# Eight row places for the projection of token blocks 2 and 3, and attention dealt out anew

## The chip, the cores and the metric

The kernel runs on one core of a Trainium2 chip. A time is device microseconds (us) of one execution. The engines are called as in the profile: PE (TensorE, matrix products), DVE (VectorE), ACT (ScalarE), POOL (GpSimd) and SP (SyncE, which here only issues DMAs). PE, DVE, ACT, POOL and SP each work off their own queue of instructions in the order in which the program puts them there. Before the change three timed runs took 1111.26, 1112.67 and 1114.58 us; their median, 1112.67 us, is the time before. The forecast is for the same median of the changed kernel.

## What is computed

A parallel transformer block on 2048 tokens of width 576. The input is normalized; sliding dilated attention (32 heads of width 18, 8 keys at distances 0, 2, ... 14) and a feed-forward network with squared ReLU (width 4608) both work on it, and both results are added to the input.

```python
def _A_ref(x, wqkv, wo):
    qkv = (x @ wqkv).reshape(B, S, 3, H, Dh)          # H = 32, Dh = 18
    ...
    idx = pos[:, None] - off[None, :]                 # off = 0, 2, ..., 14
    logits = jnp.einsum("bhsd,bhswd->bhsw", q, kg) * scale
    attn = _softmax(jnp.where(mask, logits, -1e9), axis=-1)
    o = jnp.einsum("bhsw,bhswd->bhsd", attn, vg)
    return o.reshape(B, S, D) @ wo

def _B_ref(x, w1, b1, w2, b2):
    h = jnp.einsum("bsd,df->bsf", x, w1) + b1
    r = jnp.where(h > 0, h, 0)
    return jnp.einsum("bsf,fd->bsd", r * r, w2) + b2

xn = _layernorm(x)
return x + _A_ref(xn, A_wqkv, A_wo) + _B_ref(xn, B_w1, B_b1, B_w2, B_b2)
```

## The kernel before

**Tiling.** The tokens lie in four blocks of 512 (0 to 3), the heads in four groups of 8 (0 to 3). Products in fp32 are made of high and low parts, so each operand is split by ACT (a rounded copy) and DVE (the rest). Several products are made for two blocks at once with fewer, combined products (the names `T1`, `B11`, `T2`, `T3`, `B21`, `B22`, `T4`).

**Stages.** First Q, K, V of blocks 0 and 1 (`q0`). Then `phase_a(0)`: 18 pairs of FFN tiles (`ffn_pair`, p = 0 to 17) for blocks 0 and 1, with the second FFN product and the output of block 0 between them. Then `phase_b0`: the second FFN product of block 1 (36 tiles), then Q, K, V of blocks 2 and 3, which `quad_step` makes in four halves: `(k, half)` = (0, 0), (0, 1), (1, 0), (1, 1), where k = 0 is for groups 0 and 1 and k = 1 for groups 2 and 3. Each half has 14 steps `(s, i)`, in the order of the list `steps` (L1246). The last two steps of the fourth half stand in the first FFN pair of `phase_a(1)`, as does the output of block 1 (`filler`: the functions `o_hi`, `o_lo` turn and split what attention left, `chunks` makes the products). Then `phase_a(1)` does the same as `phase_a(0)` for blocks 2 and 3, and `phase_b1` the rest of block 3.

**Rows.** A step with s = 4, 5, 6 or 7 ends with a *row*: 128 tokens of K, V and Q of one group. `row` (L1103) has ACT copy it from a PSUM bank to a place in SBUF, has DVE add a second bank where there is one (s = 4 and 6), and sends it to the DRAM tensor `kvq` of its group. There are eight rows in a half, 32 in all. The place comes from `stage`: one tile `st` with four places (`open_stage`), so that row n and row n + 4 share a place; for rows 24 to 27 a second tile, in a buffer of the name `w1r`, is added in the fourth half. A row without a second bank is sent by ACT's queue, the others by SP's, and by POOL's from row 24 on.

**Attention** of a block and group is a generator (`attention`, L403) with some 18 pieces of DVE work between its `yield`s: for four token places a product of the query with eight keys and a sum over the head's width; the softmax, whose exponential is ACT's; then for four places a product with the values and three adds. `side(k)` (L449) runs k pieces where it stands in the program. `PIECES` says how many each FFN pair of `phase_a(0)` gets after its first products; `2 + p % 2` does so in `phase_a(1)`; a tuple in `quads` (L1251) says after which steps of a half one piece stands; `complete(b)` (L470) runs pieces until block b is done.

**Slots of keys and values.** K (with 14 tokens ahead) and V of a block and group each need a buffer named `kv`, of which there are three. `offer` puts a block and group in the list, `fetch` issues the loads on POOL's queue while a slot is free, `release` gives a slot back (after the last product with K, and after the last add with V). With `kept_back` at 1 one free slot is kept: it is for `regroup(1)` (L893), which loads what attention left of block 1, regrouped by head, for the output of block 1.

**Order.** Nothing is moved by a scheduler: each engine's order is the order in which the program writes its instructions.

Of the kernel before, what the change touches and what calls it, by code (L numbers as in the profile page):

```python
# [8 lines left out]
F32 = mybir.dt.float32  # L9
# [7 lines left out]
P = 128  # L17
# [25 lines left out]
NS = 7  # L43
PLAIN = 3
ROWS = {(4 * b - 1 + k // 3, k % 3): (b, h) for b in (2, 3) for k, h in ((0, 0), (2, 2), (3, 1), (5, 2), (6, 2))}
PIECES = (0, 1, 2, 2, 2, 2, 1, 3, 2, 2, 1, 1, 1, 2, 1, 2, 3, 3)
STACK = {T1: 0, B11: 1, B22: 2, B21: 3, T3: 4, T2: 5, T4: 6}


# [1 line left out]
def block_kernel(ctx: ExitStack, tc: tile.TileContext, x, xt, wqkv, wo, w1, b1, w2, b2, w1l, out):  # L51
# [13 lines left out]
    def kv_tile(n):  # L65
        return sb.tile([P, n], F32, name="kv", bufs=3)
# [286 lines left out]
    def open_stage():  # L353
        stage[0] = sb.tile([P, 2 * NS * P], F32, name="st")[:, :NJ * QW].rearrange("p (j c) -> p j c", c=QW)
# [35 lines left out]
    def release():  # L390
        free[0] += 1
        fetch()
# [76 lines left out]

    def complete(b):  # L470
        while due(b):
            left = side(1)
            assert not left or current[0] is None

    def run(gens, k):

# [172 lines left out]
    def ffn_pair(s, p, work, first=False):  # L649
# [96 lines left out]
            w1_again(n + 1, 0) if s else combine_w1(n + 1)  # L746
        part(0)
        if not first:
            side(2 + p % 2 if s else PIECES[p], False)
        work(0)  # L750
        product(bb, T2, ss(2))
        own_w2 = first and s == 1
# [77 lines left out]
    def phase_a(s, filler):  # L830
        b = 2 * s
        ffn_pair(s, 0, filler, first=True)
        open_y(b)
        for p in range(1, NP):
            h, ops = hs.pop(s * NP + p - 1), []

            def work(i):
                if i in (0, 2):
                    ops.extend(tile_products(b, 2 * p - 2 + i // 2, h))
                add(b, ops[7 * i:7 * i + 7])  # L840

            if p == NP - 1:
                complete(b)
                regroup(b, 0)
                regroup(b, 1)
                if s == 0:
                    residual(b)
                    load_xt(2)
            ffn_pair(s, p, work)
        if s:  # L850
            residual(b)
        else:
            release()
# [12 lines left out]
        open_left(b)  # L866
        o_hi(b, 3)
        o_lo(b, 2), o_lo(b, 3)
        add(b, tile_products(b, NF - 1, h))
        w2_hi()  # L870
        w2_lo()
        o_hi(b, 4)
        o_lo(b, 4)
        side(1)
        load_h(s, 1)
        load_left(b)
        for c in range(NC):
# [207 lines left out]
    def quad_step(k, s, j, i):  # L1085
# [15 lines left out]
                nc.tensor.matmul(to, v[:, js], ws[LEFT, f][:, n], start=False, stop=n == 1, skip_group_check=True)  # L1101

        def row(n, f, x, y=None):  # L1103
            places = stage[(rows_out[0] // NJ + 1) % len(stage)]
            st = places[:, rows_out[0] % NJ]
            rows_out[0] += 1
            nc.scalar.activation(st, x, AF.Copy)
# [3 lines left out]
            (nc.scalar if y is None else nc.sync if len(stage) < 2 else nc.gpsimd).dma_start(to, st.rearrange("p (i c) -> p i c", c=CG))  # L1111

        ss = lambda n: lambda h, q: SS[n][:, h, q]
        if s == 1:
# [26 lines left out]
    def phase_b0():  # L1141
# [35 lines left out]
                nc.sync.dma_start(yscr[:, c - 1:c + 1], xr[b][0][:, c - 1:c + 1])  # L1177
        nc.sync.dma_start(yleft, kept(b, NC - 1))
        open_stage()

        def fourth_slot(k):
            split_slot(T4, raw[k, 0][:, 0])

        def hook(k, half, s, i):
# [9 lines left out]
            if half and not k:  # L1194
# [32 lines left out]
                if (s, i) == (6, 1):  # L1227
                    split_side(1, 1)
                    split_slot(B22, b22)
                    kept_back[0] = 1  # L1230
                    for g in (0, 1):
                        offer(2, g)
            if half and k:
                if (s, i) == (3, 0):
                    stage[1] = sb.tile([P, NJ, QW], F32, name="w1r", bufs=2)
                if (s, i) == (2, 1):
                    w1_again(NP, 0, nc.sync)
                if (s, i) == (5, 1):
                    complete(1)
                if (s, i) == (4, 1):  # L1240
                    w1_again(NP, 1, nc.sync)
            if kept_back[0] and not due(1):
                regroup(b, 0)
                fetch()

        steps = [(1, 0), (1, 1), (2, 0), (2, 1), (3, 0), (3, 1), (5, 0), (4, 0), (5, 1), (4, 1), (7, 0), (6, 0), (7, 1), (6, 1)]  # L1246
        def quads(k, half, some):
            for n in some:
                s, i = steps[n]
                quad_step(k, s, 2 * half + i, i)  # L1250
                if n in ((2, 3, 4, 6, 8, 10, 12), (3, 6, 8, 10, 12, 13), range(1, 14), (3, 6, 8, 10))[2 * k + half]:  # L1251
                    side(1)
                hook(k, half, s, i)

# [430 lines left out]
```

## Time and profile before

| | |
|---|---|
| timed runs | 1111.26, 1112.67, 1114.58 us |
| profiled execution, its own time | 1109.8 us |
| its span, first to last instruction | 1108.0 us |
| PE busy | 1094.3 us, 99% of the span |
| DVE busy | 879.2 us, 79% |
| ACT busy | 562.8 us, 51% |
| POOL busy | 150.0 us, 14% |
| moved by DMA | 298.97 MB, mean 270 GB/s |

The profiled execution is 1.8 us longer than its span, and lies 2.9 us below the median of the timed runs. In rows of the profile `st<-p` means that `st` is written from `p`; `p` are the PSUM banks, `pr`, `lg`, `mx`, `sm`, `q` the tiles of attention, `kvq` the DRAM tensors of K, V and Q, `o` those of attention's results. A number in brackets is the time for which the engine was idle ahead of the row, with the work that ended it. Times in rows are counted from the span's start. L118 is the helper `tt`, DVE's work on two tensors. PEld is PE's loading of weights, SPq, ACTq the DMA-issuing side of a queue.

### The profile page before, as it was taken

Reading aid. Unit: us, or ns where it says so; the run is one execution under the profiler, and the core shown is the slowest. Engines: PE = TensorE matmul, PEld = TensorE weight load, DVE = VectorE, ACT = ScalarE, POOL = GpSimd, SP = SyncE. Lnnn points to the kernel's source line nnn. Section 1 sums busy time; section 2 is a strip of 40 time slices with the busy share of each in tenths; the row PEclk is TensorE's granted clock in tenths of the full one; section 3 lists DMA queues with packets and bytes.
Section 4 is the critical chain, followed back from the end, with each engine's and each line's share of the span. In section 5 each row is a group of like instructions: output and inputs, shape, how many; then the busy total and the mean of one; then the engine's idle time right before and its main releaser. Section 6 shows DMA issues by size and latency. Waiting matters only on the chain.

```text
span 1108.0 us, 13955 instructions
## 1 busy us (share of the span) xinstructions
PE 1094.3 (99%) x4936; PEld 923.6 (83%) x4936; DVE 879.2 (79%) x1183; ACT 562.8 (51%) x794; POOL 150.0 (14%) x267
## 2 busy tenths in 40 slices
PE   9999999999999999999997999999999999999998
PEld 7998888888888888888896988888888888888887
DVE  7687988898898978999877486675767676889955
ACT  5435665656656564555343355454555545533442
POOL 4000401031130201002010300210101010101010
PEclk9999999999999999999998999999999999999999
DMA  8966998889988998876753888869586868685572
GB/s 284 334 218 220 341 404 301 321 288 261 393 278 300 341 351 284 292 252 239 268 143 120 289 322 309 296 211 332 197 316 213 289 231 309 207 289 197 186 282 88
DMA packets 109558, 298.97 MB, mean 270 GB/s; under 512 B 12648, under 2 KB 42736, under 8 KB 98608
## 3 DMA queue, kind: packets, MB, share of 16 engines
q1 hardware_dynamic: 69984, 192.84, 48.7%
q0 software_dynamic: 13200, 62.52, 16.8%
q10 hardware_dynamic: 26304, 42.71, 11.7%
q8 instruction: 39, 0.64, 0.2%
q14 instruction: 31, 0.25, 0.1%
HBM read 213.53 MB, written 84.50 MB: 269 GB/s over the span
## 4 chain that ended last, share of the span: by engine, by line
PE 88%; DVE 5%; DMA 4%; ACT 1%; issue 1%; ACTq 0%; POOL 0%; DVEq 0%; POOLq 0%
PE p L568 44%; PE p L672 34%; PE p L1097 4%; DMA kvq<-st 3%; PE p L365 2%; PE p L1101 1%; PE p L678 1%; DVE w1r L118 1%; DVE w1s L118 1%; DVE pr L118 1%; PE p L1460 1%; DVE r L118 1%; DVE lg L414 0%; DMA w2r<-in_w 0%; ACT st L357 0%
## 5 line engine op out<-in xcount | busy, mean ns | idle before, releaser
L568 PE MATMUL p<-h,w2s 128*128 128x512 f32 x2066 | 491.7, 389 | 0.3 <-ACT h L718 0.2
L568 PEld LDWEIGHTS p<-h,w2s 128*128 128x128 f32 x2066 | 387.4, 188 | 82.1 <-ACT h L718 0.6
L672 PE MATMUL p<-X,w1s 128*128 128x512 f32 x864 | 219.5, 389 | 0.2 <-DVE w1s L118 0.2
L672 PEld LDWEIGHTS p<-X,w1s 128*128 128x128 f32 x864 | 162.1, 188 | 34.0 <-DVE w1s L118 0.6
L118 DVE TENSOR_TENSOR w2s<-w2r,w2s 128x576 fp32r<-128x576 f32 x164 | 123.5, 754 | 79.5 <-ACT w2s L541 79.2
L541 ACT ACTIVATE w2s<-w2r 128x640 fp32r<-128x640 f32 x164 | 120.2, 735 | 125.9 <-PE p L568 97.9
L672 PE MATMUL p<-S,w1s 128*128 128x512 f32 x648 | 164.5, 389 | 0.0
L672 PEld LDWEIGHTS p<-S,w1s 128*128 128x128 f32 x648 | 121.6, 188 | 25.1
L443 POOL DMA_DIRECT2D o<-q x128 | 69.5, 608 | 402.8 <-DVE q L118 401.2
L714 ACT ACTIVATE r<-r,b1t 128x512 f32<-128x512 f32 x72 | 52.1, 724 | 115.4 <-DVE r L118 112.3
L118 DVE TENSOR_TENSOR pr<-q,kv 128x1152 f32<-128x1152 f32 x64 | 86.7, 1354 | 1.0 <-DVE q L118 0.2
L414 DVE TENSOR_REDUCE lg<-pr 128x64 f32<-128x1152 f32 x64 | 86.4, 1351 | 1.0
L118 DVE TENSOR_TENSOR pr<-lg,kv 128x1152 f32<-128x1152 f32 x64 | 86.6, 1353 | 0.8
L118 DVE TENSOR_TENSOR pr<-pr 128x576 f32<-128x576 f32 (+1 forms) x128 | 77.6, 607 | 3.6
L722 ACT ACTIVATE r<-r 128x1024 f32<-128x1024 f32 x72 | 76.1, 1057 | 1.2
L118 DVE TENSOR_TENSOR r<-p,r 128x512 f32<-128x512 f32 (+1 forms) x77 | 53.1, 689 | 28.5 <-ACT r L780 14.7
L118 DVE TENSOR_TENSOR h<-r,h 128x1024 fp32r<-128x1024 f32 (+3 forms) x46 | 51.8, 1136 | 18.6 <-ACT r L722 9.7
L756 ACT ACTIVATE r<-p 128x512 f32<-128x512 f32 x36 | 21.5, 598 | 80.9 <-PE p L672 80.9
L118 DVE TENSOR_TENSOR w1s<-w1r,w1s 128x1024 fp32r<-128x1024 f32 (+2 forms) x42 | 46.2, 1103 | 10.4 <-ACT w1s L510 10.0
L714 ACT ACTIVATE r<-p,b1t 128x512 f32<-128x512 f32 x72 | 48.2, 671 | 1.5 <-DMA out<-r 1.5
L118 DVE TENSOR_TENSOR h<-h 128x1024 fp32r<-128x1024 f32 x36 | 43.9, 1220 | 2.1 <-ACT h L994 2.0
L118 DVE TENSOR_TENSOR w1r<-w1r 128x256 f32<-128x256 f32 (+5 forms) x69 | 40.8, 591 | 5.4 <-ACT w1r L585 3.9
(204 smaller groups left out, 1173.8 us busy)
## 6 DMA issues: line engine op xcount, KB each, us to landing
w2r<-in_w SPq DMA_DIRECT2D x144, 320.0 KB, 4.2
kv<-kvq POOLq DMA_DIRECT2D x30, 1296.0 KB, 8.5
w<-w1s SPq DMA_DIRECT2D x21, 1024.0 KB, 8.8
w1s<-w ACTq DMA_DIRECT2D x19, 1024.0 KB, 7.5
h<-r SPq DMA_DIRECT2D x36, 512.0 KB, 7.0
h<-h SPq DMA_DIRECT2D x36, 512.0 KB, 4.1
w<-w1s SPq DMA_DIRECT2D x15, 768.0 KB, 12.1
w1s<-w ACTq DMA_DIRECT2D x15, 768.0 KB, 5.0
```

The source lines that it names most:

```text
L118: return nc.vector.tensor_tensor(out=out, in0=a, in1=b, op=op)
L365: nc.tensor.matmul(p[:, :QW], l, r, start=k == 0, stop=k == len(mm) - 1)
L414: nc.vector.tensor_reduce(out=lg[:, j * HG:(j + 1) * HG].rearrange("p a w -> p w a"), in_=pr.rearrange("p w (a d) -> p w a d", d=DH), axis ...
L443: nc.gpsimd.dma_start(rows[:, i], q[i * L:(i + 1) * L, :, a:z])
L541: nc.scalar.activation(w2s[stream[i]][:, :DE], raw2[i], AF.Copy)
L568: nc.tensor.matmul(yp[b][c], v, a, start=c not in yb[b], stop=c in last and c not in [o[0] for o in ops[i + 1:]], skip_group_check=True)
L672: nc.tensor.matmul(to, l, r, start=start and i == 0, stop=i == len(mm) - 1, skip_group_check=True)
L678: nc.tensor.matmul(to, weight(LEFT, k, f), v, start=False, stop=k == 1, skip_group_check=True)
L714: nc.scalar.activation(to, a, AF.Relu, bias=b1t[:, f:f + 1])
L722: nc.scalar.activation(r, r, AF.Square)
L756: nc.scalar.activation(u[:, 0], bb, AF.Copy)
L1097: nc.tensor.matmul(to, l[:, js], r, start=start and n == 0, stop=n == len(mm) - 1, skip_group_check=True)
```

## The change

1. **Places.** After the second FFN product of block 1, `phase_b0` takes one of the three `kv` slots as second tile of `stage`, for rows 0 to 3, 8 to 11 and 16 to 19; `st` holds rows 4 to 7, 12 to 15, 20 to 23, and 28 to 31 as before; rows 24 to 27 go to the `w1r` buffer as before. Row n and row n + 8 share a place. The queues that send the rows are as before.
2. **Slots.** One slot is kept back from the end of `phase_a(0)` to the start of the projection, so that it is there; during the projection attention has two slots, up to step (3, 0) of the fourth half, where the third is given back and `kept_back` goes to 1.
3. **Pieces.** In the third half the piece after step 2 is left out; in the fourth half the four pieces are left out, and `complete(1)` is called at step (3, 0) in place of (5, 1) alone. FFN pair 13 of `phase_a(0)` gets 0 pieces in place of 2, pair 14 gets 2 in place of 1. In `phase_a(1)` a pair gets `2 + (p > 2)` in place of `2 + p % 2`: pair 1 one less, the even pairs from 4 on one more.
4. `complete` ends with the last piece of a block; before, `side(1)` in it went on to the first piece of the next.

```diff
-PIECES = (0, 1, 2, 2, 2, 2, 1, 3, 2, 2, 1, 1, 1, 2, 1, 2, 3, 3)
+PIECES = (0, 1, 2, 2, 2, 2, 1, 3, 2, 2, 1, 1, 1, 0, 2, 2, 3, 3)
...
     def complete(b):
         while due(b):
-            left = side(1)
-            assert not left or current[0] is None
+            if current[0] is None:
+                assert not side(1)
+            else:
+                current[1] = next(current[0], "end")
+                if current[1] == "end":
+                    current[0] = None
...
-            side(2 + p % 2 if s else PIECES[p], False)
+            side(2 + (p > 2) if s else PIECES[p], False)
...
         else:
+            kept_back[0] = 1
             release()
...
-            places = stage[(rows_out[0] // NJ + 1) % len(stage)]
+            places = stage[(rows_out[0] // NJ + 1) % 2]
...
-            (nc.scalar if y is None else nc.sync if len(stage) < 2 else nc.gpsimd).dma_start(...)
+            (nc.scalar if y is None else nc.gpsimd if "last" in stage else nc.sync).dma_start(...)
...
         open_stage()
+        assert free[0]
+        free[0] -= 1
+        kept_back[0] = 0
+        stage[1] = kv_tile(NJ * QW).rearrange("p (j c) -> p j c", c=QW)
...
                     split_slot(B22, b22)
-                    kept_back[0] = 1
                     for g in (0, 1):
                         offer(2, g)
             if half and k:
                 if (s, i) == (3, 0):
-                    stage[1] = sb.tile([P, NJ, QW], F32, name="w1r", bufs=2)
+                    stage[1] = stage["last"] = sb.tile([P, NJ, QW], F32, name="w1r", bufs=2)
+                    kept_back[0] = 1
+                    free[0] += 1
+                    complete(1)
...
-            if kept_back[0] and not due(1):
+            if kept_back[0] and "last" in stage and not due(1):
                 regroup(b, 0)
                 fetch()
...
-                if n in ((2, 3, 4, 6, 8, 10, 12), (3, 6, 8, 10, 12, 13), range(1, 14), (3, 6, 8, 10))[2 * k + half]:
+                if n in ((2, 3, 4, 6, 8, 10, 12), (3, 6, 8, 10, 12, 13), (1, *range(3, 14)), ())[2 * k + half]:
                     side(1)
```

PE's order is the same in both programs, row for row. The line numbers of the changed program are up to 11 higher (L1107 is L1112 there, L1111 is L1116).

ACT, at the end of the second half and in the third: the row copies `st<-p` (L1107), the exponential `lg<-lg` (L423) of the attention of block 1, group 0, and the copies between banks (L1116, L1121). Before:

```order
L1107 ACTIVATE st<-p_4850 128x432
L122 ACTIVATE r_5172<-mb 128x432
L122 ACTIVATE h<-w1r 128x2x432
L1116 ACTIVATE p_4838<-p_4837 128x432
L1116 ACTIVATE p_4849<-p_4848 128x432
L1121 ACTIVATE p_4840<-p_4838 128x432
L423 ACTIVATE lg<-lg 128x256
L1121 ACTIVATE p_4851<-p_4849 128x432
L1107 ACTIVATE st<-p_4837 128x432
L1111 DMA kvq_98<-st 128x3x144
L1107 ACTIVATE st<-p_4838 128x432
```

The changed program there:

```order
L1112 ACTIVATE st<-p_4849 128x432
L122 ACTIVATE r_5173<-mb 128x432
L122 ACTIVATE h<-w1r 128x2x432
L1121 ACTIVATE p_4837<-p_4836 128x432
L1121 ACTIVATE p_4848<-p_4847 128x432
L1126 ACTIVATE p_4839<-p_4837 128x432
L1126 ACTIVATE p_4850<-p_4848 128x432
L423 ACTIVATE lg<-lg 128x256
L1112 ACTIVATE kv<-p_4836 128x432
L1116 DMA kvq_98<-kv 128x3x144
L1112 ACTIVATE kv<-p_4837 128x432
```

The exponential stands one copy later, straight ahead of the third half's first row copies, and those go to the `kv` tile.

DVE, in the third half: the end of the softmax, and the first of the row adds (from the bank of step (4, 0)) among the products with the values. Before:

```order
L425 TENSOR_REDUCE sm<-lg 128x32
L426 RECIPROCAL sm<-sm 128x32
L118 TENSOR_TENSOR lg<-lg,sm 128x256
L118 TENSOR_TENSOR pr<-lg,kv 128x1152
L118 TENSOR_TENSOR st<-p_4839,st 128x432
```

The changed program there:

```order
L425 TENSOR_REDUCE sm<-lg 128x32
L426 RECIPROCAL sm<-sm 128x32
L118 TENSOR_TENSOR lg<-lg,sm 128x256
L118 TENSOR_TENSOR kv<-p_4838,kv 128x432
L118 TENSOR_TENSOR pr<-lg,kv 128x1152
```

The row add has moved ahead of the product with the values, and so have the three that follow it.

POOL, from the end of `phase_a(0)` to the fourth half, tiles with their numbers: Q, K and V loads of group 1 and group 0 (`kvq1`, `kvq0`), the stores of attention's results of block 1 (`o10`, `o11`). The tiles `q_3841`, `kv_3840`, `kv_4712` are Q, K, V of block 1, group 0 before; `q_5195`, `kv_5194` are Q and K of block 2, group 0. Before:

```order
L387 DMA kv_3731<-kvq1_97 128x2592
L443 DMA o10_102<-q_3062 128x1x96 x4
L443 DMA o11_103<-q_3062 128x1x48 x4
L385 DMA q_3841<-kvq0_96 128x576
L387 DMA kv_3840<-kvq0_96 128x2592
L607 DMA stk1_152<-st_4232 32x4x128 x14
L387 DMA kv_4712<-kvq0_96 128x2592
L443 DMA o10_102<-q_3494 128x1x96 x4
L443 DMA o11_103<-q_3494 128x1x48 x4
L385 DMA q_5195<-kvq0_96 128x576
L387 DMA kv_5194<-kvq0_96 128x2592
```

The changed program there:

```order
L443 DMA o10_102<-q_3140 128x1x96 x4
L443 DMA o11_103<-q_3140 128x1x48 x4
L387 DMA kv_3838<-kvq1_97 128x2592
L611 DMA stk1_152<-st_4228 32x4x128 x14
L385 DMA q_4709<-kvq0_96 128x576
L387 DMA kv_4708<-kvq0_96 128x2592
L443 DMA o10_102<-q_3570 128x1x96 x4
L443 DMA o11_103<-q_3570 128x1x48 x4
L387 DMA kv_4998<-kvq0_96 128x2592
L385 DMA q_5196<-kvq0_96 128x576
L387 DMA kv_5195<-kvq0_96 128x2592
```

Each load stands later: V of block 1, group 0 (`kv_4712` before, `kv_4998` now) is behind the stores of group 1's results, and K of block 2 (`kv_5195`) waits there for the slot of K of block 1, group 0.

More of the change, by code (lines that the diff above doesn't have):

```diff
@@ L1110, in row @@
             to = kvq[gs[f]][:, PAD + n * TB:PAD + (n + 1) * TB].rearrange("i (p j) c -> p j i c", j=NJ)[:, j]
-            (nc.scalar if y is None else nc.sync if len(stage) < 2 else nc.gpsimd).dma_start(to, st.rearrange("p (i c) -> p i c", c=CG))
+            (nc.scalar if y is None else nc.gpsimd if "last" in stage else nc.sync).dma_start(to, st.rearrange("p (i c) -> p i c", c=CG))
         ss = lambda n: lambda h, q: SS[n][:, h, q]
```

## The prediction

> **What bounds the kernel now.** I read first the page's busy times, then who PE waited for, then PE's busy time over the halves of the projection, then the chain of waits at the one place where it falls. Page, and the list of PE's waits (us in total, times, longest us):
>
> ```profile
> span 1108.0 us, 13955 instructions
> PE 1094.3 (99%) x4936; PEld 923.6 (83%) x4936; DVE 879.2 (79%) x1183; ACT 562.8 (51%) x794; POOL 150.0 (14%) x267
> ...
> PE p L1097 <- ACT st L1107: 7.2, 1, 7.2
> PE p L1377 <- DVE lg L1370: 2.1, 1, 2.1
> PE p L568 <- ACT h L718: 0.2, 1, 0.2
> PE p L672 <- DVE w1s L118: 0.2, 1, 0.2
> ```
>
> PE is the bound, and 13.7 us of the span are all that it isn't busy. Of these 2.1 lie at the start, and 7.2 in one wait for a row copy of the projection. PE's order isn't changed, so the change can gain or lose only by PE's waits. The halves of the projection, from the first matmul of one to that of the next (PE busy in the second column, then PEld, DVE, ACT, POOL, the granted clock, DMA share, GB/s):
>
> ```profile
> 542.70:562.28 19.58, 19.58 (x101) 18.82 (x100) 15.40 (x23) 7.32 (x13) 0.00 (x0) 1.00 0.76 244
> 562.28:581.86 19.58, 19.58 (x101) 18.82 (x100) 16.32 (x19) 10.40 (x18) 5.45 (x10) 1.00 0.42 113
> 581.86:610.41 28.55, 21.30 (x102) 20.02 (x101) 21.05 (x30) 8.61 (x17) 0.00 (x0) 0.88 0.36 114
> ```
>
> Three halves with the same matmuls: two take 19.58 us, the third 28.55. The excess, 28.55 - 19.58 = 8.97 us, is more than the wait of 7.2: the clock granted in the third is 0.88, and PE is busy 21.30 us for work of 19.58. A stall of 7.25 us and 1.72 us at a lower clock after it make the 8.97. Where it comes from, by the chain of waits (start, length, what) and the timeline there:
>
> ```profile
> 579.12 0.60 DVE st L118
> ...
> 579.74 12.37 DMA kvq<-st
> ...
> 592.21 0.54 ACT st L1107
> ...
> 578.44 0.57 POOL L385 DMA_DIRECT2D q<-kvq  x1 [9.68 <-DMA kvq<-st]
> 579.00 0.56 POOL L387 DMA_DIRECT2D kv<-kvq  x1
> 581.47 0.93 ACT L122 ACTIVATE h<-w1r 128x864 fp32r<-128x864 f32 x1 [0.44 <-ACT st L1107]
> 582.30 0.55 ACT L122 ACTIVATE r<-mb 128x432 fp32r<-128x432 f32 x1
> 585.58 0.60 DVE L118 TENSOR_TENSOR r<-mb,r 128x432 fp32r<-128x432 f32 x1
> 592.78 0.61 DVE L118 TENSOR_TENSOR st<-p,st 128x432 f32<-128x432 f32 x1 [6.60 <-ACT st L1107]
> 592.80 5.24 PE L1097 MATMUL p<-w1s,S 128*128 128x432 f32 x18 [7.25 <-ACT st L1107]
> ```
>
> Row 11 is finished by DVE at 579.72 and sent at 579.74, behind the loads of Q and K that POOL issued at 578.44 and 579.00; it lands 12.37 us later. Row 15 uses the same place of `st`, so its copy, which ACT comes to at 582.85 behind two splits, starts at 592.21; it is the copy that empties the bank which PE's next product overwrites. DVE, too, stands idle for 6.60 us.
>
> **Part 1, the places: -8.97 us.** With a reuse distance of eight, row 15 waits for row 7. That was finished here:
>
> ```profile
> 563.90 0.60 DVE L118 TENSOR_TENSOR st<-p,st 128x432 f32<-128x432 f32 x1
> ```
>
> Sent at 564.5, it would have to take over 18 us to hold a copy at 582.85; the slow one took 12.37. Row 23 follows row 15 by one half, 19.58 us: the same margin. So the wait goes, and with it the low clock. Taken away whole: 8.97 us.
>
> The Trainium skill (TensorE: Matmul & The Clock Gate, Part 1: The HAM clock gate) says that an idle window of about 3.4 us halves the clock, and about 3.4 us of busy time restore it; by that rule the ramp costs 1.7 us, as the rows have it, and waits under some 3 us left by the change would cost no ramp.
>
> **Part 2, DVE and ACT in the third half: 0 to +0.3 us.** PE comes 8.97 us earlier, DVE only the 6.60 that it stood idle: the add of row 15 follows the row of 585.58 at once. So against PE, DVE is 2.4 us later in the third half than before. Who waits for it:
>
> ```profile
> 599.75 0.42 ACT L423 ACTIVATE lg<-lg 128x256 f32<-128x256 f32 x1 [2.34 <-DVE lg L118]
> 600.52 0.51 ACT L1107 ACTIVATE st<-p 128x432 f32<-128x432 f32 x1
> 601.53 0.53 ACT L1107 ACTIVATE st<-p 128x432 f32<-128x432 f32 x1 [0.50 <-PE p L1097]
> 604.14 1.33 PE L1097 MATMUL p<-h,X 128*128 128x432 f32 x6
> 614.80 0.31 DVE L118 TENSOR_TENSOR q<-pr 128x144 f32<-128x144 f32 x1
> ```
>
> The exponential waits for DVE, and two row copies are queued behind it on ACT; the second empties the bank of the product at 604.14 (step (7, 0)). Now: exponential at 599.75 - 6.60 = 593.15, ending at 593.57; the copy between banks that followed it is done earlier, so the first row copy starts then, the second 1.01 after it, as here (594.58), and ends at 595.11. PE comes to (7, 0) at 604.14 - 8.97 = 595.17. That holds by 0.06 us; I charge 0 to 0.3 and take 0.1. The row adds stand ahead of the products with the values now, so the later steps have more room than this one.
>
> **Part 3, what attention left of block 1 comes later: 0 to +4 us.** The attention of block 1, group 0 ends at 615.11 before; now at 615.11 - 6.60 and 0.2 more (the moved add, due at 594.9, waits for the copy that ends at 595.11), so 608.7. PE's shift would have put it at 606.1: it is 2.6 us late. Behind it stand the results' stores, the load of V, the regrouping load, the turning, and chunk 0 of block 1's output on PE. Timeline, and the landing times of the regrouping loads:
>
> ```profile
> 622.29 0.54 POOL L901 DMA_DIRECT2D kv<-o  x1 [0.57 <-DMA o<-q]
> ...
> DMA to landing us min/median/max: 12.0/13.8/15.5
> ...
> 637.85 1.30 DVE L925 STREAM_TRANSPOSE r<-kv 128x512 f32<-128x512 f32 x2 [0.64 <-DMA kv<-o]
> 639.31 1.14 ACT L926 ACTIVATE h<-r 128x512 fp32r<-128x512 f32 x2
> 641.58 12.86 PE L568 MATMUL p<-h,w2s 128*128 128x512 f32 x56
> ...
> 620.00:640.00 20.00, 20.00 (x97) 17.86 (x96) 6.99 (x10) 7.40 (x14) 5.24 (x8) 1.00 1.03 354
> ```
>
> The first load is issued 7.18 us after attention's end and takes 15.5 us, with all DMA engines full (share 1.03). Now: issued at 615.9; at the same 15.5 it lands at 631.4, and one turn (0.65) and one split (0.57) later, at 632.6, PE has what it needs. PE comes there at 641.58 - 8.97 = 632.61. Lower bound: the load finds fewer transfers ahead of it, since those that PE triggers moved by 8.97, and lands up to 2.6 us earlier: no wait. Upper bound: the longest landing of a row's store, 19.6 us (quoted below), so a wait of 4.1. I take 0.2, nearest to this load's own 15.5.
>
> The skill (DMA: Bandwidth & Descriptors, Queues, rings and completion order) says that each DMA engine takes its queues in turn, packet by packet. By it POOL's queue keeps its share however late the load is issued, and lands in the same 15.5 us; the sum stays.
>
> **Part 4, loads with two slots: 0.** V of group 0 can only be loaded once V of group 1 is done with:
>
> ```profile
> 567.70 1.07 POOL L443 DMA_DIRECT2D o<-q  x2 [0.15 <-issue]
> 621.16 0.56 POOL L387 DMA_DIRECT2D kv<-kvq  x1 [1.41 <-DMA o<-q]
> ...
> 601.50 1.36 DVE L118 TENSOR_TENSOR pr<-lg,kv 128x1152 f32<-128x1152 f32 x1
> ...
> DMA to landing us min/median/max: 5.6/8.8/17.6
> ...
> DMA to landing us min/median/max: 2.1/4.0/19.6
> ```
>
> The stores end at 568.77; the load follows by 570.2 (POOL's wait of 1.41 at the same place of the next attention, 621.16), and by the landing times of all such loads (first of the two rows; the second is the rows' stores) it lands between 575.8 and 587.8. DVE needs it at 601.50 - 6.60 and, behind the moved add (0.2 and 0.6), so at 595.7: 7.9 us of room at the worst. Row stores that it now runs beside are waited for by nobody for eight rows. K of block 2 waits for the slot of K of block 1, and is first read in the next FFN pair, behind the turned results of 632. V of group 1 and K of group 0 are loaded during block 1's second FFN product, long before use.
>
> **Part 5, the other pieces: 0.** Pieces in FFN pairs 13 and 14 move by two at most, 2.7 us at 1.36; PE waits on DVE in no pair there (0.2 us in all, above). In `phase_a(1)` seven even pairs get a piece more. Four pairs of 17.4 us, DVE's busy time alone:
>
> ```profile
> 700.00:717.45 17.45, 11.42 (x12) 1.00 0.88 311
> 717.45:734.90 17.45, 12.18 (x17) 1.00 0.75 271
> 734.90:752.40 17.50, 12.24 (x15) 1.00 0.63 210
> 752.40:769.80 17.40, 11.42 (x12) 1.00 0.91 322
> ```
>
> Over 5 us of each are free, so a piece of 1.36 fits, and odd pairs have three already. Without that cover it would be 7 x 1.36 = 9.5 us.
>
> **Sum.** -8.97 + 0.1 + 0.2 = -8.67 us. The profiled execution took 1109.8, so 1101.1; the median of the runs is 2.9 above that, and I put the gain on the median: 1112.67 - 8.67 = 1104.0.
>
> **The rivals.**
>
> *A, given back at chunk 0.* The regrouping load lands late, by part 3's upper bound: PE idles 4.1 us there and, if the ramp is paid again, 1.7 more. Net gain 8.67 + 0.2 - 5.8 = 3.1, so 1109.6; half of it, 1106.9, is the middle. For: two steps without slack, and DMA full. Against: the transfers it competes with start 8.97 us earlier. Chance 0.16, of it 0.03 below the 0.3% mark.
>
> *B, slower: DVE stuck for V of group 0.* Every row add and the exponential are queued behind that product on DVE. From 595.7 on, after some 0.8 us of slack (taken small), each us that V lands later is a us of PE. To be past the old time by 0.3% (3.3 us) it must cost 12.0, so land after 608.5, 38 us after its issue; the longest such landing is 17.6. For: it runs beside eight row stores, and one store took 12.37 beside such a load. Time 1116 or more. Chance 0.05.
>
> *C, DVE becomes the bound in `phase_a(1)`.* 9.5 us back: 1113.5, no difference. For: three pieces ahead of the first products. Against: the free 5 us. Chance 0.05.
>
> *D, the wait isn't taken away but moves to another place* (to a store of over 18 us; the longest seen took 19.6): 1112.7. Chance 0.03.
>
> **Numbers.** Forecast 0.71, of it all faster. About 0.3% is what can be told from no change here, so the marks are 1109.3 and 1116.0. Faster: 0.71 + 0.13 of A = 0.84 and 0.01 of C; same: 0.03 of A, 0.04 of C, 0.03 of D; slower 0.05. Range: below, the 2.9 us by which the timed runs exceed the profiled one may be the same wait, longer: 1104.0 - 2.9 = 1101.1, so 1101.0. Above, to most of A: 1109.3. Outside it lie B, C, D and the end of A, under 0.2.
>
> **What would show it.** Right: no wait of PE on L1112 (the row copy) in the list of PE's waits; a third half of 19.6 to 20 us at clock 1.00; PE's idle time near 5 us. Part 2 wrong: a wait of PE on a row copy at step (7, 0). Part 3 wrong: the transposes waiting for `kv<-o` and PE's L568 idle for the split `h`. B: DVE idle on `kv<-kvq`. C: PE idle in pairs of `phase_a(1)`. A span above 1103 with none of these would mean that I have missed a wait.

## The result and the profile after

Six runs of the changed kernel took 1102.19 to 1103.72 us, median **1102.55 us**; six of the kernel before beside them 1110.51 to 1114.58, median 1111.38. The ratio is 0.9917 (95% interval 0.9904 to 0.9930): faster by 0.8%. The profiled execution of the changed kernel took 1102.89 us, with a span of 1101.2. PE's busy time on its page, and the list of its waits (us in total, times, longest us):

```profile
span 1101.2 us, 13948 instructions
PE 1093.1 (99%) x4936; PEld 923.2 (84%) x4936; DVE 879.5 (80%) x1183; ACT 562.2 (51%) x794; POOL 149.0 (14%) x267
```

```profile
PE p L1388 <- DVE lg L1381: 2.1, 1, 2.1
PE p L676 <- DVE w1s L118: 1.3, 1, 1.3
PE p L676 <- ACT w1s L514: 0.8, 1, 0.8
```

The wait of 7.2 us for a row copy has no successor in the list: L1112, the row copy, is not in it. The wait of 2.1 at the start is as before. New are 0.8 and 1.3 us, both for `w1s` (the split weights of the first FFN product), near 93 us, in code that the change doesn't touch; before, 0.2 stood there. So the span fell by 1108.0 - 1101.2 = 6.8 us only, though the third half of the projection has all of the forecast. The first three halves of the projection by windows, each from its first matmul to the next half's (columns as in the prediction):

```profile
545.29:564.88 19.59, 19.59 (x102) 18.82 (x100) 17.04 (x26) 7.42 (x13) 0.00 (x0) 1.00 0.80 254
564.88:584.46 19.58, 19.58 (x101) 18.83 (x100) 14.79 (x16) 10.39 (x18) 5.41 (x10) 1.00 0.56 169
584.46:604.04 19.58, 19.58 (x101) 18.82 (x100) 18.57 (x26) 8.46 (x17) 0.53 (x1) 1.00 0.53 169
```

28.55 us became 19.58 with PE busy throughout at clock 1.00: 8.97 us. The projection starts at 545.29 where it started at 542.70 before; of the 2.59 us between, 1.93 are the longer waits for `w1s` (2.08 for 0.15), the rest was lost elsewhere ahead of it. To set a time of this profile beside one that the prediction worked out, 2.59 is to be taken off.

The timeline around the exponential (prediction: 593.15, now 595.64 - 2.59 = 593.05), ACT's rows first and PE's step (7, 0) last:

```profile
595.64 0.42 ACT L423 ACTIVATE lg<-lg 128x256 f32<-128x256 f32 x1 [3.41 <-DVE lg L118]
595.96 0.51 ACT L1112 ACTIVATE kv<-p 128x432 f32<-128x432 f32 x1
...
596.97 0.96 ACT L1112 ACTIVATE kv<-p 128x432 f32<-128x432 f32 x2 [0.50 <-ACT kv L1112]
...
597.78 1.33 PE L1102 MATMUL p<-h,X 128*128 128x432 f32 x6
```

PE's row has no bracket: it doesn't wait. And what follows the attention of block 1, group 0, on DVE, POOL, DVE, ACT and PE:

```profile
610.96 0.31 DVE L118 TENSOR_TENSOR q<-pr 128x144 f32<-128x144 f32 x1
...
611.56 4.33 POOL L443 DMA_DIRECT2D o<-q  x8 [17.43 <-DVE q L118]
617.74 0.56 POOL L387 DMA_DIRECT2D kv<-kvq  x1 [1.86 <-issue]
622.29 0.54 POOL L906 DMA_DIRECT2D kv<-o  x1 [3.98 <-DMA o<-q]
...
631.47 1.31 DVE L930 STREAM_TRANSPOSE r<-kv 128x512 f32<-128x512 f32 x2 [0.66 <-DMA kv<-o]
...
632.35 1.14 ACT L931 ACTIVATE h<-r 128x512 fp32r<-128x512 f32 x2
...
635.19 12.86 PE L572 MATMUL p<-h,w2s 128*128 128x512 f32 x56
```

Chunk 0 has no wait either. The first split, which takes half of the 1.14, is done near 632.92, and PE comes 2.27 us later.

### The profile page after: what moved, and what is told of

The parts are those of the page before. It is cut to its first block, busy times and chain, and to the rows that moved or that the text cites. A ratio compares the mean times of both kernels' runs of the same rounds, so it can differ in the third digit from the quotient of the medians.

```text
span 1101.2 us, 13948 instructions
## 1 busy us (share of the span) xinstructions
PE 1093.1 (99%) x4936; PEld 923.2 (84%) x4936; DVE 879.5 (80%) x1183; ACT 562.2 (51%) x794; POOL 149.0 (14%) x267
## 4 chain that ended last, share of the span: by engine, by line
PE 94%; DVE 3%; DMA 1%; issue 1%; ACT 1%; ACTq 0%; POOL 0%; DVEq 0%; POOLq 0%
PE p L572 47%; PE p L676 35%; PE p L1102 6%; PE p L365 3%; PE p L1106 1%; PE p L1471 1%; DMA kvq<-st 1%; PE p L682 1%; DVE w1r L118 1%; DVE pr L118 0%; PE p L1388 0%; DVE r L118 0%; DVE S L118 0%; DVE w1s L118 0%; ACT st L357 0%
```

## The experiments

Eleven runs in three groups, each group on one chip beside runs of the kernel before. Its median there was 1112.85 us (13 runs, 1109.72 to 1118.04; the first four kernels below), 1113.73 (11 runs, 1108.04 to 1118.43; the next four) and 1114.55 (13 runs, 1110.62 to 1117.59; the last three). Line numbers of some variants differ by one from those of the changed kernel.

### The kernel before, a second profile (`before_again`)

No edit.

> The kernel before, profiled once more. The median of its runs lies 1.6 to 2.9 us above its first profile, while the changed kernel's profile has a wait of 2.1 us (0.8 and 1.3) on w1s at the first FFN product near 93 us, in code that the change leaves alone. Theory 'start': that early wait comes and goes between executions; this profile shows it at 1 to 3 us and a span near 1110. Rival 'projection': the early part is the same in every execution and the stall for the row copy is longer instead, 9 to 10 us in place of 7.25. In both the third half takes 28 us or more.

Measured: 1115.47 us, span 1113.8, so a slower execution than the first profile's. PE's waits in it, and ACT's rows ahead of the second of them (an ACTq row is ACT's issue of a DMA):

```profile
PE p L1097 <- ACT st L1107: 5.8, 1, 5.8
PE p L672 <- ACT r L756: 2.7, 1, 2.7
PE p L1377 <- DVE lg L1370: 2.1, 1, 2.1
PE p L672 <- DVE w1s L118: 1.3, 1, 1.3
```

```profile
633.56 4.30 ACTq L1111 DMA_DIRECT2D kvq<-st  x1
637.91 0.60 ACT L756 ACTIVATE r<-p 128x512 f32<-128x512 f32 x1 [4.38 <-issue]
```

The row copy's wait is shorter than in the first profile (5.8 against 7.2), and the third half the same:

```profile
585.78:614.16 28.38, 22.63 (x101) 21.23 (x100) 22.03 (x32) 8.76 (x17) 0.00 (x0) 0.88 0.36 110
```

28.38 - 19.58 = 8.80 us. What makes this execution 5.8 us longer than the first profiled one lies elsewhere: 1.3 us for `w1s` near 94 us, and 2.7 us in the first FFN pair, where ACT was held 4.30 us by issuing one row's store, with a clock of 0.50 and 0.67 in the four microseconds behind it. So the wait for `w1s` is in both kernels; the change didn't bring it. The theory 'start' is right in that, though its span near 1110 was 3.8 us too short; the rival 'projection' falls, since the stall was shorter and not 9 to 10 us.

### Four places, the rest of the change kept (`four_places`)

```diff
-            places = stage[(rows_out[0] // NJ + 1) % 2]
+            places = stage[1 if "last" in stage and rows_out[0] // NJ == 6 else 0]
...
-        stage[1] = kv_tile(NJ * QW).rearrange("p (j c) -> p j c", c=QW)
```

> The changed kernel with its two slots, its later loads and its dealing of pieces, but rows 0 to 23 all in the four places of st, as before. Theory 'places': row 15 still waits for row 11's store, whose landing of 12.37 us is due to a full queue of stores; the stall of 7 us at the third half comes back and the time is that of before, 1110 to 1112. Rival 'loads': row 11's store was slow only because the load of K of block 2, group 0 ran beside it; that load now stands 14 us later, the store lands in 4 to 6 us, and PE waits 0 to 2 us: 1102.5 to 1105.

Measured: 1110.03 us (10 runs, 1107.02 to 1112.3), ratio to before 0.9969 (0.9953 to 0.9985). PE's wait, the third half, and the store that ended the wait, by the waits, the windows and the chain:

```profile
PE p L1102 <- ACT st L1112: 4.3, 1, 4.3
```

```profile
587.61:613.49 25.88, 21.54 (x102) 19.85 (x102) 20.68 (x31) 8.74 (x17) 0.00 (x0) 0.93 0.37 115
```

```profile
583.14 9.47 DMA kvq<-st
```

The wait is back with the four places: 25.88 - 19.58 = 6.30 us are lost in the third half, so without the change's tile and all that it brings, row 15 waits for row 11 again. But 6.30 is less than the 8.97 and 8.80 of the kernel before, and the median is 1112.85 - 1110.03 = 2.8 us better than its: the rest of the change seems to do something of its own. Row 11's store takes 9.47 us here, 12.37 and 10.87 there, though it is issued at the same place, with the loads of Q and K at the same places ahead of it. The last three runs take this up.

The run doesn't decide between 'places' and 'loads', since its edit brings back more than the places. POOL's load of K of block 2, which the expectation took to stand later in this kernel, is issued ahead of row 11's store again. In the changed kernel the load waits for a slot. POOL's row here, and then in the changed kernel:

```profile
582.35 0.53 POOL L387 DMA_DIRECT2D kv<-kvq  x1
```

```profile
593.59 0.53 POOL L387 DMA_DIRECT2D kv<-kvq  x1 [12.03 <-DVE pr L118]
```

Row 11's store in the changed kernel, sent at 582.3 without that load beside it:

```profile
DMA to landing us min/median/max: 4.7/4.7/4.7
```

That is the 4 to 6 us which the rival names. The table at the end of the experiments shows that four places cover a store of 5.1 us. So two things that the changed kernel does would each take the wait away, as an estimate from these figures: row 15 waits for row 7 and no longer for row 11, and row 11's store is no longer slow. No run has the one without the other.

### All pieces dealt as before (`old_pieces`)

```diff
-PIECES = (0, 1, 2, 2, 2, 2, 1, 3, 2, 2, 1, 1, 1, 0, 2, 2, 3, 3)
+PIECES = (0, 1, 2, 2, 2, 2, 1, 3, 2, 2, 1, 1, 1, 2, 1, 2, 3, 3)
...
-            side(2 + (p > 2) if s else PIECES[p], False)
+            side(2 + p % 2 if s else PIECES[p], False)
...
-                if n in (..., (1, *range(3, 14)), ())[2 * k + half]:
+                if n in (..., range(1, 14), (3, 6, 8, 10))[2 * k + half]:
```

> The changed kernel with eight places and two slots, but all pieces dealt as before (FFN pairs 13 and 14, the third and fourth half, 2 + p % 2); complete(1) still at step (3, 0). Theory: the dealing is worth nothing by itself but keeps ACT and DVE in time in the third half, where the prediction found 0.06 us of room; with a piece more after step 2 the exponential comes at the same place in ACT's order as before and the row add behind a product with the values, so PE waits 0 to 1 us: 1102.5 to 1104. Rival: the dealing carries part of the gain; with the old one PE waits in the third half, at chunk 0 or in the FFN pairs for 3 us or more: above 1105.5.

Measured: 1102.56 us (4 runs, 1101.85 to 1103.2), ratio 0.9899 (0.9875 to 0.9923). The third half:

```profile
585.82:605.75 19.93, 19.91 (x101) 18.58 (x100) 19.03 (x27) 7.08 (x15) 0.53 (x1) 1.00 0.48 157
```

0.35 us more than 19.58, and no wait for a row copy. The median is that of the changed kernel, 1102.55: the new dealing gives nothing that the medians can show.

### The pieces of FFN1 alone dealt as before (`old_ffn_pieces`)

The first two of the three edits above.

> The changed kernel with the pieces of the FFN pairs dealt as before (pairs 13 and 14, and 2 + p % 2), those of the halves as changed. Theory: DVE has over 5 us free in each pair, so the time is that of the changed kernel within 1 us, 1102 to 1103.5, with no wait of PE in a pair. Rival: attention of blocks 2 comes late for the end of the second FFN stage and complete(2) holds PE up: 1104 or more.

Measured: 1103.47 us (4 runs, 1101.15 to 1104.86), ratio 0.9905 (0.9878 to 0.9933); PE waits 1.3 and 0.9 us for `w1s` and nowhere in `phase_a(1)`. No difference again that four runs spread over 3.7 us could show.

### A second tile of places for block 0 too (`q0_places`)

In the changed kernel's projection of block 0, ACT's copies wait for stores four rows earlier, as those of blocks 2 and 3 did. The slot kept back there serves for four more places.

```diff
-    def qkv_out(b, g, j, p):
-        nc.scalar.activation(stage[0][:, j], p[:, :QW], AF.Copy)
+    def qkv_out(b, g, j, p, tile=0):
+        nc.scalar.activation(stage[tile][:, j], p[:, :QW], AF.Copy)
...
-            qkv_row(b, g, j, r % 5)
+            qkv_row(b, g, j, r % 5, 1 if r < 16 and r // 4 % 2 == 0 else 0)
...
+        stage[1] = kv_tile(NJ * QW).rearrange("p (j c) -> p j c", c=QW)
```

> The changed kernel, with a second tile of four places for the first 16 rows of the projection of block 0 as well (the slot that is kept back there), so that ACT's row copies there no longer wait for a store four rows earlier. Theory 'early stores': the waits of PE in the first FFN product, near 93 and 95 us (0.8 and 1.3 us in the profile of the changed kernel), come from those copies: ACT is held for 5.1 us at 54.4 us, and DVE's chain behind it, down to the values that are split for w1s, is late. Then they go: 0 to 0.3 us of waits there, span 1099.2, the median 2 us below that of the changed kernel (about 1100.5). Rival 'load': w1s is late because of its own load or because DVE has its whole work ahead of it anyway: the waits of 1.3 and 0.8 us stay, span 1101 to 1102, no difference in the medians.

Measured: **1100.19 us** (6 runs: 1099.66 to 1100.55 and one of 1103.37), ratio to before 0.9884 (0.9859 to 0.9909). The span of the profiled run is 1098.8 us, and this is the whole list of PE's waits:

```profile
PE p L1388 <- DVE lg L1381: 2.1, 1, 2.1
```

The waits for `w1s` are gone. What moved, on ACT and DVE, first in the changed kernel's profile and then in this one:

```profile
54.40 0.53 ACT L357 ACTIVATE st<-p 128x432 f32<-128x432 f32 x1 [5.08 <-DMA kvq<-st]
...
56.41 1.09 DVE L118 TENSOR_TENSOR w1r<-w1r 128x896 fp32r<-128x896 f32 x1 [6.44 <-ACT w1r L589]
57.42 1.35 DVE L118 TENSOR_TENSOR pr<-q,kv 128x1152 f32<-128x1152 f32 x1
```

```profile
54.24 0.53 ACT L357 ACTIVATE kv<-p 128x432 f32<-128x432 f32 x1 [0.76 <-PE p L365]
...
53.51 1.09 DVE L118 TENSOR_TENSOR w1r<-w1r 128x896 fp32r<-128x896 f32 x1 [3.11 <-ACT w1r L589]
54.52 1.35 DVE L118 TENSOR_TENSOR pr<-q,kv 128x1152 f32<-128x1152 f32 x1
```

ACT no longer stands 5.08 us for a store, DVE's attention of block 0 starts 2.90 us earlier, and `w1s` is ready when PE comes. The theory 'early stores' holds. Against the changed kernel in the same job it is 1102.14 - 1100.19 = 1.95 us; the two ratios' intervals overlap, since the runs of before spread by ten, but five of these six runs lie below all six of the changed kernel. It beats both kernels.

### The changed kernel again (`after_again`)

No edit.

> The changed kernel itself, beside the others on one chip. Both theories: 1102.6 us, within 1101.5 and 1103.7; waits of PE of 1.3 to 2.1 us for w1s near 94 us, none for a row copy, third half of the projection 19.6 us, and a landing of the first regrouping load after 7 to 10 us. If the 2.9 us by which the timed runs of the kernel before exceed its profile had come from the row copies' wait, no run of this one would show such spread: a spread of under 2 us over the runs; if it comes from waits elsewhere, some runs of this kernel show it too, up to 1105.

Measured: 1102.14 us (6 runs, 1101.29 to 1105.18), ratio 0.9903 (0.9875 to 0.9931). In the profiled run PE waits 1.3 and 0.4 us for `w1s`, and the first regrouping load lands after 9.1 us. The spread is 3.9 us, over the 2 us which the one reading allowed, so the spread of the kernel before need not come from the row copies. The two longest runs, 1105.18 and 1104.05, are those with a mean clock of 0.998; the other four, 1101.29 to 1102.38, have 0.999 or 1.000.

### DVE late ahead of the exponential (`dve_late`)

```diff
-            nc.vector.tensor_reduce(out=lg[:, j * HG:(j + 1) * HG]...
+            for _ in range(3 if (b, g, j) == (1, 0, NJ - 1) else 1):
+                nc.vector.tensor_reduce(out=lg[:, j * HG:(j + 1) * HG]...
```

> The changed kernel; the last sum of the logits of block 1, group 0 is done three times over (same result), so DVE is 2 x 1.35 = 2.70 us later from there on. Part 2's theory: the exponential and the two row copies behind it on ACT come 2.7 us later, PE waits at step (7, 0) of the third half for the row copy: 2.70 less a room of 0.3, so 2.4 us; the third half takes 22.0, and nothing is lost at the output of block 1 behind it, since PE is then as late as DVE: span +2.4. Rival: DVE's lateness is taken up by idle time ahead of the exponential (room of over 2 us): no wait of PE on a row copy, span the same.

Measured: 1106.81 us (one run), span 1105.1. PE's step (7, 0) and its whole list of waits:

```profile
600.93 1.44 PE L1103 MATMUL p<-h,X 128*128 128x432 f32 x6 [2.39 <-ACT kv L1113]
```

```profile
PE p L1103 <- ACT kv L1113: 2.4, 1, 2.4
PE p L1389 <- DVE lg L1382: 2.1, 1, 2.1
PE p L677 <- DVE w1s L118: 1.3, 1, 1.3
PE p L573 <- DVE S L980: 0.4, 1, 0.4
PE p L677 <- ACT w1s L515: 0.3, 1, 0.3
```

2.70 us more on DVE cost PE 2.39 at the place that part 2 names, so the room there is 0.31 us. The third half took 22.24 us, where 22.0 was expected. No wait for the split `h` at chunk 0. Of the other 1.5 us that this span has above that of the changed kernel, most were lost near 94 us, far ahead of the edit; that place is shown in the last section.

### Attention's end late (`values_late`)

```diff
-            tt(pr.rearrange("p w (a d) -> p w a d", d=DH), at[...]...
-               shifted(v, j, [DH, HG], [1, DH]), ALU.mult)
+            for _ in range(4 if (b, g, j) == (1, 0, NJ - 1) else 1):
+                tt(pr.rearrange("p w (a d) -> p w a d", d=DH), at[...]...
+                   shifted(v, j, [DH, HG], [1, DH]), ALU.mult)
```

> The changed kernel; the last product with the values of block 1, group 0 is done four times over (same result), so attention ends 3 x 1.35 = 4.05 us later (at 615.3 in place of 611.3), in a stretch where DVE has idle time. Part 3's theory: the regrouping load is issued 4.05 later and takes the same time, so its values reach PE 4.05 later; PE has 2.3 us of room at chunk 0 (split done at 632.9, PE there at 635.2): PE waits 1.8 us on chunk 0 (the split h), span +1.8. Rival: the load's time depends on what stands ahead of it, and one issued later meets fewer transfers, as between the kernel before and the changed one (issued 3.8 us later than reckoned, landed when reckoned): it lands at most 2.3 later, and PE doesn't wait.

Measured: 1105.47 us (one run), span 1103.8. The transposes, PE at chunk 0, and the time to landing of the regrouping loads (KB, us):

```profile
634.33 1.30 DVE L931 STREAM_TRANSPOSE r<-kv 128x512 f32<-128x512 f32 x2 [4.84 <-DMA kv<-o]
...
635.76 9.60 PE L573 MATMUL p<-h,w2s 128*128 128x512 f32 x41 [1.73 <-ACT h L932]
```

```profile
kv<-o POOLq DMA_DIRECT2D x1, 768.0 KB, 9.3
```

4.05 us more on DVE cost PE 1.73, with 1.8 forecast from the room of 2.27. The load took 9.3 us, as in the changed kernel (9.2): one issued later doesn't land faster. The rival falls. (The span is 2.6 us above that of the changed kernel; what isn't this wait lies in waits of 0.2 to 0.3 us elsewhere and in PE's busy time, and one run doesn't tell more.)

### Four places, two slots, and all pieces as before (`four_old`)

The edit of the four places and the three of the pieces, together.

> Four places as before the change and all pieces dealt as before it: what is left of the change are the two slots, with the load of V of block 1, group 0 behind the results of group 3 of block 0 instead of 40 us earlier. It is to tell where the 2.8 us come from by which the kernel with four places and the rest of the change (1110.03) is faster than the kernel before (1112.85). Theory 'slots': they come from the later load; this kernel takes 1109 to 1111 too. Theory 'pieces': they come from the new dealing; it takes 1112 to 1114, as the kernel before. Both: PE waits for a row copy in the third half, by the time of row 11's store less 5.1 us (12.37 and 7.25, 10.87 and 5.75, 9.47 and 4.34 in the three profiles so far).

Measured: 1110.24 us (10 runs, 1107.91 to 1111.82), ratio to before 0.9957 (0.9943 to 0.9972). The theory of the slots holds as far as the medians go: without the new dealing the gain that the four places left is there, 1114.55 - 1110.24 = 4.3 us in this group, and the pieces give nothing here either. What this kernel still has of the change is the order of the loads, with V of block 1, group 0 some 40 us later (POOL issues it at 570.90, for 528.98 before), and `complete(1)` at step (3, 0). K of block 2 is loaded where it was (581.01): nothing holds the third buffer here.

### Four places again, and the kernel before a third time (`four_again`, `before_third`)

No edit beyond those shown.

> The kernel with four places and the rest of the change again, for a second profile. If the rest of the change makes row 11's store itself faster, the store takes 9 to 10 us again and the wait is near 4.3; if its time only varies from run to run, it may take anything between 9.5 and 12.4, with a wait of 4.3 to 7.3. In both cases the wait is the store's time less 5.1.

> The kernel before, a third profile. Row 11's store takes 10.9 to 12.4 us if its time belongs to this kernel, or 9 to 10 if it only varies; PE's wait for the row copy is the store's time less 5.1 us.

Measured: 1110.76 and 1113.89 us (one run each). From the chain and PE's timeline of the second profile with four places:

```profile
581.10 10.92 DMA kvq<-st
```

```profile
592.70 5.98 PE L1102 MATMUL p<-w1s,S 128*128 128x432 f32 x18 [5.79 <-ACT st L1112]
```

And of the third profile of the kernel before, ACT's longest issue of a row in the first FFN pair, and PE behind it:

```profile
632.13 4.10 ACTq L1111 DMA_DIRECT2D kvq<-st  x1
```

```profile
636.93 2.42 PE L672 MATMUL p<-S,w1s 128*128 128x512 f32 x6 [2.47 <-ACT r L756]
```

All six profiles with four places side by side (us; the third half's loss is its length less 19.58, taken between the same matmuls of two halves; the last two columns are of the first FFN pair):

| profile | row 11's store | PE's wait for the copy | third half's loss | ACT's longest issue of a row | PE's wait for ACT |
|---|---|---|---|---|---|
| before, first | 12.37 | 7.25 | 8.97 | under 1 | 0 |
| before, second | 10.87 | 5.75 | 8.80 | 4.30 | 2.67 |
| before, third | 10.50 | 5.38 | 7.57 | 4.10 | 2.47 |
| four places | 9.47 | 4.34 | 6.30 | 1.25 | 0 |
| four places, again | 10.92 | 5.79 | 8.24 | 2.05 | 0.4 |
| four places, old pieces | 9.67 | 4.55 | 7.42 | 2.96 | 1.3 |

The wait is the store's time less 5.12 us in every row, to 0.01: the store alone sets it, and four places cover a store of 5.1 us. The store's time varies from 9.5 to 12.4 us, and its ranges with and without the rest of the change overlap (the third profile's 10.50 lies between the two ranges that were expected), so that the two slots make this store faster isn't shown. In all six the load of K of block 2 is issued 0.7 to 0.8 us ahead of the store. In all seven profiles with eight places that load comes some 11 us behind the store, and the store takes 4.6 to 5.0 us. The stores of rows 12 and 13, from the same tile `st` in both kinds, go from 8.3 to 11.2 and 6.6 to 9.4 us to 4.1 to 4.4 and 2.4 to 2.7. So the load beside them, and not the tile, is what goes with the slow stores. What the later loads gain may lie behind the third half: ACT's issue of a row in the first FFN pair takes 1.3 to 3.0 us in place of 4.1 to 4.3, and PE waits 0 to 1.3 us for ACT in place of 2.5 to 2.7 in two of three profiles of before. Behind these two waits the clock fell as well (last section, 1.7 us lost each time), so they cost 4.4 and 4.2 us in all, about what the medians show; but the first profile of before has neither the long issue nor the wait, so this isn't shown. In all seven profiles with eight places that wait is zero.

## Why the prediction was right

1102.55 us lies in the range, 1.45 below the 1104.0 forecast. Step by step:

**Part 1, the places.** The wait and the low clock behind it went whole, -8.97 us in the profile, as put. Row 15's copy waits for nothing. That the wait was for row 11's store is confirmed by the table: a store's time less 5.12 us. That the places took it away is not shown. The prediction put the slow store down as given, and put the later load of K at 0 in part 4; but with that load gone from beside it the store takes 4.6 to 5.0 us, which four places cover by their 5.12, if only by 0.1 to 0.5 us. Eight places would cover 12.4 us too. Which of the two is needed stays open: it would take four places with the late load, or eight with the early one. The size was that of one profile, the largest of the three of before (7.57 to 8.97).

**Part 2, DVE and ACT.** The times came out within 0.1 us (exponential 593.05 for 593.15). The charge of 0.1 was 0; the room of 0.06 is 0.31, measured by `dve_late`. The chain is the one named, DVE's sums, exponential, two row copies, step (7, 0).

**Part 3, what attention left of block 1.** Attention's end was put at 608.7 and came at 611.27 - 2.59 = 608.68. Two of its later terms were wrong, in opposite directions. The first load was put 7.18 us behind attention's end and was issued 622.29 - 611.27 = 11.02 behind it: POOL waited 3.98 us for the results' stores, where before it waited 0.57. And it took 9.2 us to land where 15.5 were put. Together it is in time by 2.27 us, where none was left by the sum. The landing times of this load:

```profile
kv<-o POOLq DMA_DIRECT2D x1, 768.0 KB, 9.2
```

In the kernel before it took 15.5, 17.8 and 17.7 us, with four places 15.0 to 16.7, and in the six other profiles with eight places 9.0 to 12.1. It was slow in the six profiles in which PE had waited for row 15's copy, and not in `dve_late`, where PE waited 2.39 us at step (7, 0). Why is open: no run changed only the traffic beside it. The Trainium skill (DMA: Bandwidth & Descriptors, Queues, rings and completion order) says that a DMA engine takes its queues in turn, from which the prediction concluded that the load keeps its 15.5 us. The runs don't bear out that conclusion; of the turns themselves they show nothing.

**Part 4, two slots.** No wait for V in any profile with two slots, as put. But they weren't worth 0: with four places the later load of V gains 2.8 to 4.3 us by the medians. And where the load of K waits for a slot, as put, row 11's store is fast; the prediction reckoned nothing for that. With eight places what the slots gain can't be told from what the places gain, since the second tile lies in the third slot.

**Part 5, the pieces.** 0, as put; with all of them dealt as before the median is the same, 1102.56.

**The rivals.** A's place is real, with a room of 2.27 us and a price of one for one beyond it (`values_late`), but nothing used the room up. B, C and D show no wait in the changed kernel's list.

**What was wrong.** First, the note on the 2.9 us by which the timed runs of before exceed its profile: "may be the same wait, longer". That wait is the longest in the first profile. In the two others, 4.1 and 5.7 us longer in their own time, it is shorter, and there are 1.3 us for `w1s` near 94 us and 2.5 to 2.7 us for ACT's issue in the first FFN pair. The first profile had neither of them by chance; the prediction, made from it alone, missed both. The first is in both kernels: 11 of the 13 profiles of all kernels wait 1.3 us there, with up to 0.9 more. The second is one that the change takes away beside what was reckoned. So -8.67 is near the 8.83 of the medians, 1111.38 - 1102.55, in part by luck: the third half lost less than 8.97 in the other two profiles, and a wait that wasn't reckoned went too. The two profiles differ by 6.8, and the later groups' medians by some 10 to 12 (1112.85 - 1102.56, with the pieces as before; 1113.73 - 1102.14). Second, "a span above 1103" as the sign of a missed wait was set too high: the span was 1101.2 with a missed wait of 2.1 in it. Third, "PE's idle time near 5 us": measured 1101.2 - 1093.1 = 8.1. From the prediction's own rows it should have read 13.7 - 7.25 + 0.3 = 6.8, since 1.72 of the 8.97 us is busy time at a low clock. With the 0.3 not needed, and 2.1 us for `w1s` in place of the two waits of 0.2 before, that makes 13.7 - 7.25 - 0.4 + 2.1 = 8.2.

## What to carry to other kernels

Where a copy that frees a PSUM bank waits for a store some places back, the distance of reuse must cover the slowest store beside the loads of that stage, not the median one, or the load that slows the store must be moved; where an edit does both, as here, test each alone. Look for every other stage with the same ring of places, for the same edit paid there again (1.95 us at the kernel's start). To forecast what a shorter wait brings, work out for each engine what it alone gains, and test the room at the next step by repeating an instruction: two such runs gave the two margins to 0.1 us. One profile of the kernel before is a sample: of three, the first had one wait at its longest and lacked two others.

## What the runs showed of the hardware

**A large load issued just ahead of a small store goes with a slow store.** Row 11's store of 216 KB took 9.5 to 12.4 us in the six profiles in which a load of 1296 KB was issued 0.7 to 0.8 us ahead of it on another queue, and 4.6 to 5.0 us in the seven in which it was not.

**Issuing a DMA can hold an engine for microseconds.** ACT's issue of a row's store takes 0.37 us in nearly all rows. With the DMA share at 0.94 to 1.02, one took 4.30 and, in another execution, 4.10 us, and PE waited 2.67 and 2.47 us for the ACT work queued behind it. Why the issue is held the trace doesn't show.

**Short waits can cost clock.** The prediction said that waits under some 3 us would cost no ramp. In `dve_late` the stall of 2.39 us cost none: the granted clock of that half is 1.00. But behind the waits of 2.67 and 2.47 us for ACT in the second and third profile of before it fell to 0.50, and near 94 us, where PE idled 0.30 and 1.27 us, the clock halved. PE's windows near 94 us in `dve_late`, then in the changed kernel:

```profile
94.47:95.10 0.63, 0.63 (x3) 0.54 (x4) 0.63 (x1) 0.28 (x1) 0.00 (x0) 1.00 0.11 31
95.10:95.50 0.40, 0.40 (x3) 0.30 (x2) 0.40 (x1) 0.00 (x0) 0.00 (x0) 0.53 0.83 328
...
96.00:97.00 1.00, 1.00 (x4) 0.81 (x3) 1.00 (x2) 0.52 (x1) 0.00 (x0) 0.50 1.09 434
...
98.50:99.00 0.50, 0.50 (x4) 0.45 (x3) 0.43 (x3) 0.00 (x0) 0.00 (x0) 0.96 0.89 186
```

```profile
96.00:98.00 2.00, 2.00 (x10) 1.66 (x9) 2.00 (x3) 0.58 (x1) 0.00 (x0) 1.00 0.99 381
```

Half speed for some 3.4 us, so 1.7 us lost, more than the waits themselves; in the changed kernel, which idled 0.80 and 1.28 us at the same place, nothing. Behind the waits of 2.67 and 2.47 us, too, the windows give 1.7 us lost. Of the eleven profiles that wait there for `w1s`, the clock fell in three (`dve_late`, `four_places`, `old_ffn_pieces`). The Trainium skill (TensorE: Matmul & The Clock Gate, Part 1: The HAM clock gate) calls the window of some 3.4 us free-running, not tied to the kernel's start. That it depends on where in the window a wait falls would fit a drop in some executions and none in others, and the 3.4 us at half speed agree; that the window must be idle, as the page states it, doesn't agree with a drop after 1.57 us of idle time in two parts. After the row copy's wait, too, the clock's share of the loss varies: 8.97 - 7.25 = 1.72 us in the first profile of before, 8.80 - 5.75 = 3.05 in the second. The longer runs of the changed kernel, with a mean clock of 0.998, fit such drops too (1.7 of 1100 us is 0.0015), but have no trace to show it.
